# Modulation and c gradients of an adaLN block, taken from TensorE to ScalarE and VectorE

## The chip, the cores and the metric

The kernel runs on one core of a Trainium2 chip. The metric is device time in microseconds (us) of that core from launch to end; the median of three runs is compared. A separate, profiled execution gives the trace. Engines are named as in the profile: PE (TensorE matmuls; PEld its weight loads), DVE (VectorE), ACT (ScalarE), POOL (GpSimd), SP (the engine whose queue issues most DMAs).

## The reference

A transformer block with conditioning: a vector c gives six modulation rows, which shift, scale and gate an attention part and a dense part. The kernel computes the block's output and the gradients of nine inputs.

```python
mod = (silu(c) @ w_mod).reshape(1, 6, 1, 512)      # c 1x512, w_mod 512x3072
sa, ca, ga, sb, cb, gb = mod[:, 0..5]
h = layernorm(x) * (1 + ca) + sa
x = x + ga * attention(h, wqkv, wo)                # 2048 tokens, 32 heads of 16
h = layernorm(x) * (1 + cb) + sb
x = x + gb * dense(h, w1, b1, w2, b2)              # relu(.)^2, width 1792
out, vjp = jax.vjp(f, x, wqkv, wo, w1, b1, w2, b2, c, w_mod); grads = vjp(grad_out)
```

All inputs and outputs are bf16. What matters here are the last two gradients. With dmod the gradient of the six modulation rows (3072 numbers: sums over all tokens),

- the gradient of w_mod is the outer product silu(c)^T dmod, 512 x 3072 (out_9), and
- the gradient of c is silu'(c) * (w_mod dmod^T), 512 numbers (out_8).

## The kernel before, in words

Tokens are tiled by 128 (TT = 16 tiles), the width 512 by 128 (DC = 4). Most stages run under a schedule written out by hand: the order of instructions on PE, ACT and DVE is the program's own. In the last stage this holds for these three engines, while the order of SP's queue is made by the framework's scheduler. SP issues its DMAs in order; a DMA that has to wait for a semaphore holds all DMAs behind it. SP's DMAs also take turns on eight semaphores, so a DMA can't be issued before the eighth one ahead of it has landed.

The stages:

1. `prep` (lines 845 to 984, the first 41 us): loads, layer norm statistics, modulation columns, first keys and queries, four value tiles. Here SP also turns w_mod: `wmod_turn` (L911) issues four transposing DMAs of 128x512 for each of the first four sixths of w_mod into `tmpT`, and `wmod_store` (L917) writes them to the DRAM tile `wmT_st`. A row of c, its sigmoid and its product go to `rows_st` (L847, L867, L981 to L983).
2. Forward attention with exp on ACT (`ET`, L562), in units of four score matmuls and two ACTIVATEs. Tasks are hung on units: in the first twelve, `value_tile` (L815), which evicts a projection to `vP` on DVE (L822). `vP` has two buffers of four tiles, each written to `v_st` when full (L825), so tile t needs the store of tiles t-8 to t-5 to have landed. `later_stage` (L665) does weight turns at every fourth unit; for i of 30 and 31 the last two sixths of w_mod. At i = 25 the reciprocals of the two scale rows are stored to `rows_st`.
3. Dense part of the forward pass and its gradients, whose row sums over tokens end in `rows_st` rows 2 to 5 (L1533).
4. Attention gradients (most of the second half).
5. The last stage (from L1770, some 125 us): it turns the gradients of q, k, v to tokens (L1936), runs `dh1(t)` for 16 token tiles (12 matmuls, then DVE reductions, L1873), `row_sums(t)` (two matmuls against ones, L1893) and `dx_out(t)` (L1897), and then 12 products `dwqkv(b, ic)` of 16 matmuls each (L1906).

The gradients of w_mod and c are spread through stage 5. The late four rows (j = 2 to 5) come from `rows_st`, the first two (j = 0, 1) from the row sums after the last tile. `mod_cols` (L1838) turns each row of dmod into columns by four 1x1 matmuls. `c_grad` (L1845) multiplies those columns with the turned w_mod on PE, four matmuls a row. `wmod_grad` (L1850) makes the outer product on PE, a matmul with one contracted row for each 128x512 block, evicted by ACT into `dwms` and stored by SP.

Of the kernel before, what the change touches and what calls it, by code (L numbers as in the profile page):

```python
# [14 lines left out]
AF = mybir.ActivationFunctionType  # L15
ALU = mybir.AluOpType
AX = mybir.AxisListType
BF = dt.bfloat16
# [16 lines left out]
def kernel(  # L35
# [46 lines left out]
    rows_st = dram.tile([11, D], F32, name="rows_st")  # L82
# [15 lines left out]
    wmT_st = dram.tile([6, P, 4, D], BF, name="wmT_st")  # L98
# [48 lines left out]
    with ExitStack() as ph:  # L147
# [29 lines left out]
        def sp(to, fro, transpose=False):  # L177
            SP.dma_start(out=to, in_=fro, transpose=transpose)  # L178

        def later(lag, f, *args):  # L180
            due.append((unit[0] + lag, f, args))
# [483 lines left out]
        def later_stage(i):  # L665
# [22 lines left out]
            if i >= 26:  # L688
                j = i - 26
                wT = tmpT[:, 4 * (j % 2):4 * (j % 2) + 4, :]  # L690
                for q in range(4):
                    sp(wT[:, q, :], w_mod[:, (4 * j + q) * P:(4 * j + q + 1) * P], True)
                later(3, sp, wmT_st[j], wT)
                return
            if i == 25:
                for r, j in enumerate((1, 4)):
                    DVE.reciprocal(racc[0:1, r, :], modbc[0:1, j, :])
                later(3, sp, rows_st[9:11, :].unsqueeze(0), racc[0:1, 0:2, :])
                return
# [145 lines left out]
        def prep():  # L845
            cbf, crows = racc[0:1, 3, 0:256].bitcast(BF), racc[0:1, 0:3, :]
            sp(c_col, c.rearrange("o (ic p) -> p (o ic)", p=P))  # L847
            sp(cbf, c[0:1, :])
# [18 lines left out]
            ACT.activation(crows[:, 1, :], cbf, AF.Sigmoid)  # L867
# [43 lines left out]
            def wmod_turn(j):  # L911
                for q in range(4):
                    sp(tmpT[:, 4 * (j % 2) + q, :], w_mod[:, (4 * j + q) * P:(4 * j + q + 1) * P], True)
                if j > 0:
                    wmod_store(j - 1)

            def wmod_store(j):  # L917
                sp(wmT_st[j], tmpT[:, 4 * (j % 2):4 * (j % 2) + 4, :])

            for j in range(4):  # L920
                wmod_turn(j)
            wmod_store(3)
# [58 lines left out]
            POOL.tensor_copy(crows[:, 0, :], cbf)  # L981
            POOL.tensor_tensor(crows[:, 2, :], crows[:, 0, :], crows[:, 1, :], ALU.mult)
            sp(rows_st[6:9, :].unsqueeze(0), crows)  # L983
# [786 lines left out]
    with ExitStack() as ph:  # L1770
# [4 lines left out]
        psw = ph.enter_context(tc.tile_pool(name="psJw", bufs=2, space=bass.MemoryType.PSUM))  # L1775
        psk = ph.enter_context(tc.tile_pool(name="psK", bufs=1, space=bass.MemoryType.PSUM))
# [21 lines left out]
        def row(i):  # L1798
            r = big.tile([1, D], F32, name="row", tag="row", bufs=5)
            SP.dma_start(out=r[:], in_=rows_st[i:i + 1, :])  # L1800
            return r

        load_x(0)
        rows = {i: row(i) for i in (2, 5, 3, 4, 10)}
        load_x(1)
        wmodT = {}

        def load_wmodT(j):
            wmodT[j] = big.tile([P, 4, D], BF, name="wmodT", tag="wmodT", bufs=3)
            SP.dma_start(out=wmodT[j][:], in_=wmT_st[j])  # L1810
# [7 lines left out]
        siluc_rowbf = big.tile([1, D], BF, name="siluc_rowbfK")  # L1818
        dfac = big.tile([1, D], F32, name="dfac")
        dmodbf = big.tile([1, 6, D], BF, name="dmodbf")  # L1820
        dmodT = big.tile([P, 24], BF, name="dmodT")
        pdc = psk.tile([P, D], F32, name="pdc", tag="pdc")
        pc = psk.tile([P, 24], F32, name="pcolK", tag="pcolK")

        def silu_rows():
            DVE.tensor_copy(siluc_rowbf[:], rows[8][:])
            DVE.tensor_scalar(dfac[:], rows[7][:], -1.0, 1.0, ALU.mult, ALU.add)
            DVE.tensor_tensor(dfac[:], rows[6][:], dfac[:], ALU.mult)
            DVE.scalar_tensor_tensor(out=dfac[:], in0=dfac[:], scalar=1.0, in1=rows[7][:], op0=ALU.add, op1=ALU.mult)

        def mod_grad_rows(js, srcs):
            for j, src in zip(js, srcs):
                if j in (2, 5):
                    DVE.tensor_copy(dmodbf[:, j, :], src)
                else:
                    DVE.tensor_tensor(dmodbf[:, j, :], src, rows[9 if j < 2 else 10][:], ALU.mult)

        def mod_cols(js):  # L1838
            for j in js:
                for q in range(4):  # L1840
                    PE.matmul(pc[:, 4 * j + q:4 * j + q + 1], dmodbf[0:1, j, q * P:(q + 1) * P], ones_bf[0:1, 0:1],
                              start=True, stop=True)
            DVE.tensor_copy(dmodT[:, 4 * js[0]:4 * js[-1] + 4], pc[:, 4 * js[0]:4 * js[-1] + 4])

        def c_grad(j, first, last):  # L1845
            for q in range(4):
                PE.matmul(pdc[0:1, :], dmodT[:, 4 * j + q:4 * j + q + 1], wmodT[j][:, q, :],
                          start=(first and q == 0), stop=(last and q == 3))

        def wmod_grad(js, ic, lo, hi, pool, tag):  # L1850
            dwm = dwms[:, ic % 2]
            for i, j in list(enumerate(js))[lo:hi]:
                pw = pool.tile([P, D], F32, name="pwm", tag=tag)
                PE.matmul(pw[:], siluc_rowbf[0:1, ic * P:(ic + 1) * P], dmodbf[0:1, j, :], start=True, stop=True)
                ACT.activation(dwm[:, i, :], pw[:], AF.Identity)
            if hi < len(js):
                return
            SP.dma_start(out=out_9[ic * P:(ic + 1) * P, js[0] * D:(js[-1] + 1) * D].rearrange("p (j d) -> p j d", d=D),
                         in_=dwm[:, 0:len(js), :])

        dwms = stg.tile([P, 2, 4, D], BF, name="dwms", tag="dQacc", bufs=1)
        late_js = (2, 3, 4, 5)
# [30 lines left out]
        def row_sums(t):  # L1893
            for acc, src in zip(rsums, dxs[t]):
                PE.matmul(acc[0:1, :], ones_bf[:, 0:1], src[:], start=(t == 0), stop=(t == TT - 1))
# [31 lines left out]
        with tc.manual_schedule(engines={PE.engine, ACT.engine, DVE.engine}):  # L1927
# [17 lines left out]
            mod_grad_rows(late_js, [rows[j][:] for j in late_js])  # L1945
# [3 lines left out]
            for t in range(TT):  # L1949
                if t % 2 == 0 and t >= 2 and t // 2 + 2 < TT // 2:  # L1950
                    load_x(t // 2 + 2)
                if t in (0, 1, 2, 4, 6, 7):
                    load_wmodT({0: 2, 1: 3, 2: 4, 4: 5, 6: 0, 7: 1}[t])
                if t in (8, 9, 10, 11):
                    load_h1(t - 8)
                if t + 1 < TT:
                    norm_tile(t + 1)
                dh1(t)
                if t > 0:
                    row_sums(t - 1)  # L1960
                    dx_out(t - 1)
                if t == 0:
                    for i in (8, 7, 6, 9):
                        rows[i] = row(i)
                if t == 4:
                    silu_rows()
                if t == 1:
                    mod_cols(late_js)
                if 3 <= t < 7:
                    c_grad(t - 1, t == 3, False)  # L1970
                if 7 <= t < 15:
                    wmod_grad(late_js, (t - 7) // 2, 2 * ((t - 7) % 2), 2 * ((t - 7) % 2) + 2, psw, "pw")
            for b in range(3):
                for ic in range(DC):
                    dwqkv(b, ic)
                    i = b * DC + ic
                    if i == 0:
                        row_sums(TT - 1)
# [8 lines left out]
                    if i == 6:  # L1987
                        dcbf = wk.tile([1, D], BF, name="dcbf", bufs=1)
                        DVE.tensor_tensor(dcbf[:], pdc[0:1, :], dfac[:], ALU.mult)
                        SP.dma_start(out=out_8[0:1, :], in_=dcbf[:])  # L1990
# [61 lines left out]
```

## Time and profile before

| what | us |
|---|---|
| median of 3 runs | 2512.56 (2511.92 to 2516.4) |
| profiled execution, span | 2513.8 |
| PE busy | 2335.0 (93%) |
| ACT busy | 2302.6 (92%) |
| DVE busy | 1809.7 (72%) |
| POOL busy | 348.0 (14%) |
| start until the first `ET` | 41.71 |
| last stage, first `dh1` matmul to last product's last matmul | 2403.7 to 2510.0 |

The page's parts: busy time of each engine; the span in 40 slices; DMA queues; the chain of work that ended last, followed back from the last instruction to what released each step; groups of instructions with their mean duration and the idle time before them; DMA issues. The chain and the timeline can be asked for in a window of time. A line of the timeline has start, duration, engine, line, operation, output <- input, shapes, count, and in brackets the idle time of that engine just before, with what ended it. "SPq" is SP's queue while it issues or waits. Matmul durations in the trace are latencies: 128x512 matmuls show 0.38 us but follow each other by 0.216 us.

### The profile page before, as it was taken

Reading aid. Unit: us, or ns where it says so; the run is one execution under the profiler, and the core shown is the slowest. Engines: PE = TensorE matmul, PEld = TensorE weight load, DVE = VectorE, ACT = ScalarE, POOL = GpSimd, SP = SyncE. Lnnn points to the kernel's source line nnn. Section 1 sums busy time; section 2 is a strip of 40 time slices with the busy share of each in tenths; the row PEclk is TensorE's granted clock in tenths of the full one; section 3 lists DMA queues with packets and bytes.
Section 4 is the critical chain, followed back from the end, with each engine's and each line's share of the span. In section 5 each row is a group of like instructions: output and inputs, shape, how many; then the busy total and the mean of one; then the engine's idle time right before and its main releaser. Section 6 shows DMA issues by size and latency. Waiting matters only on the chain.

```text
span 2513.8 us, 49777 instructions
## 1 busy us (share of the span) xinstructions
PE 2335.0 (93%) x18916; PEld 777.9 (31%) x19005; DVE 1809.7 (72%) x2317; ACT 2302.6 (92%) x3577; POOL 348.0 (14%) x370
## 2 busy tenths in 40 slices
PE   7898889989988998999999999999999999999999
PEld 3232223222322323442233322233222323222343
DVE  6555153455435454579999999999998999999872
ACT  7999999999999999539999999999999999999952
POOL 2000000210333142210111101011010110110100
PEclk9999999999999999999999999999999999999999
DMA  6476465356748765969999999999999999999972
GB/s 203 129 193 177 136 131 139 96 160 136 110 88 174 153 131 118 264 211 184 207 203 210 199 198 204 204 201 206 204 200 206 199 195 204 206 199 215 197 254 72
DMA packets 1220981, 447.15 MB, mean 178 GB/s; under 512 B 1096951, under 2 KB 1191607, under 8 KB 1220486
## 3 DMA queue, kind: packets, MB, share of 16 engines
q1 hardware_dynamic: 1192822, 409.11, 81.8%
q0 software_dynamic: 10944, 16.78, 4.5%
q10 hardware_dynamic: 16976, 18.07, 2.8%
q8 instruction: 149, 2.44, 0.4%
q14 instruction: 90, 0.74, 0.1%
HBM read 96.75 MB, written 73.95 MB: 68 GB/s over the span
## 4 chain that ended last, share of the span: by engine, by line
PE 40%; ACT 39%; issue 7%; DVE 7%; DMA 4%; SPq 2%; ACTq 1%; POOL 0%; DVEq 0%; another core or an unknown queue 0%
ACT E_u L1601 24%; ACT ET L562 11%; PE dqacc L1682 5%; PE psST L560 4%; PE psS_A L1595 3%; PE pm L233 3%; PE accVK L1655 2%; ACT dsT L1761 2%; PE oacc L576 2%; PE psS_B L1595 2%; SPq L178 2%; PE psS_C L1595 2%; PE pm L412 2%; PE pdh L1876 2%; PE pwq L1910 2%
## 5 line engine op out<-in xcount | busy, mean ns | idle before, releaser
L1617 DVE TENSOR_TENSOR dS_u<-psD_u,E_u 128x1024 bf16<-128x1024 f32 x1024 | 1186.2, 1219 | 71.2 <-PE psD_u L1615 25.5
L562 ACT ACTIVATE ET<-psST 128x1024 bf16<-128x1024 f32 x1024 | 942.3, 1247 | 25.3 <-PE psST L560 24.7
L1601 ACT ACTIVATE E_u<-psS_A 128x512 bf16<-128x512 f32 x768 | 509.6, 664 | 11.0 <-PE psS_C L1595 8.5
L1601 ACT ACTIVATE E_u<-psS_B 128x512 bf16<-128x512 f32 x768 | 502.6, 654 | 12.5 <-PE psD_u L1615 3.4
L1615 PE MATMUL psD_u<-iv,ido 32*128 32x512 bf16 x2048 | 409.9, 388 | 0.5 <-DVE dS_u L1617 0.2
L560 PE MATMUL psST<-qt_sb,kt_sb 32*128 32x512 bf16 x2048 | 316.5, 387 | 53.0 <-ACT ET L562 46.2
L1601 ACT ACTIVATE E_u<-psS_C 128x512 bf16<-128x512 f32 x512 | 333.7, 652 | 2.7 <-PE psS_B L1595 1.0
L1595 PE MATMUL psS_B<-ik,iq 32*128 32x512 bf16 x768 | 294.9, 384 | 12.5 <-ACT E_u L1601 5.0
L1595 PE MATMUL psS_A<-ik,iq 32*128 32x512 bf16 x768 | 293.4, 382 | 11.1 <-DVE dwlast L237 1.0
L1595 PEld LDWEIGHTS <-iq 32*128 32x128 bf16 x2048 | 130.5, 91 | 316.0 <-issue 299.9
L1655 PE MATMUL accVK<-dS_u,qz 128*32 128x512 bf16 x2048 | 213.0, 390 | 0.5 <-PE psD_u L1615 0.3
L576 PE MATMUL oacc<-ET,vaug 128*32 128x512 bf16 x2048 | 207.8, 396 | 1.9 <-DVE ostage L580 1.9
L1664 PE MATMUL accVK<-E_u,dOs_tok 128*16 128x512 bf16 x2048 | 203.7, 386 | 0.0
L1700 POOL TENSOR_TENSOR dQacc<-dQacc,dqtmp 128x512 f32<-128x512 f32 x64 | 81.3, 1271 | 851.4 <-ACT dqtmp L1695 851.4
L1595 PE MATMUL psS_C<-ik,iq 32*128 32x512 bf16 x512 | 194.6, 380 | 4.2
L560 PEld LDWEIGHTS <-kt_sb 32*128 32x128 bf16 x2048 | 85.4, 91 | 341.0 <-issue 320.4
L1682 PE MATMUL dqacc<-dsT,KS_tok 128*32 128x512 bf16 x2048 | 147.7, 387 | 18.7 <-DMA dsT<-dS_u 4.3
L1761 ACT ACTIVATE dsT<-ptT 128x1024 bf16<-128x1024 bf16 x128 | 145.3, 1135 | 7.0 <-PE ptT L1645 6.4
L251 DVE COPY part<-pm 128x512 f32<-128x512 f32 (+2 forms) x103 | 63.5, 617 | 117.5 <-PE pm L233 106.0
L1615 PEld LDWEIGHTS <-ido 32*128 32x128 bf16 x2048 | 105.0, 91 | 100.7 <-issue 94.5
L1655 PEld LDWEIGHTS <-qz 128*32 128x32 bf16 x2048 | 58.5, 94 | 177.8 <-issue 162.8
L576 PEld LDWEIGHTS <-vaug 128*32 128x32 bf16 x2048 | 53.0, 93 | 121.0 <-issue 121.0
(407 smaller groups left out, 2499.5 us busy)
## 6 DMA issues: line engine op xcount, KB each, us to landing
p_st<-part POOLq DMA_DIRECT2D x36, 256.0 KB, 5.2
kt_sb<-qkT_st SPq DMA_DIRECT2D x124, 64.0 KB
wA<-in_B_w_dram SPq DMA_DIRECT2D x28, 256.0 KB
wB<-w1T_st SPq DMA_DIRECT2D x21, 256.0 KB
wA<-w2T_st SPq DMA_DIRECT2D x21, 256.0 KB
wB<-in_B_w_dram SPq DMA_DIRECT2D x21, 256.0 KB
p_st<-part POOLq DMA_DIRECT2D x25, 192.0 KB, 4.2
p_st<-part SPq DMA_DIRECT2D x18, 256.0 KB
```

Of the source, the lines that this page charges most:

```text
L560: PE.matmul(ps[:, hi, :], kt_sb[r:r + 32, kt * P:(kt + 1) * P], qt_sb[r:r + 32, :], start=True, stop=True, tile_position=(r, 0))
L562: ACT.activation(ET[:, 2 * pair:2 * pair + 2, :], ps[:], AF.Exp, scale=SCALE)
L576: PE.matmul(oacc[32 * hq:32 * hq + 32, :], lhsT, ET[:, hq, :], start=(kt == 0), stop=(kt == TT - 1), tile_position=(0, 32 * hq), skip_grou ...
L1595: PE.matmul(psS[:], st["q"][r:r + 32, qt * P:(qt + 1) * P], st["k"][r:r + 32, kc * 512:kc * 512 + 512], start=True, stop=True, tile_positi ...
L1601: ACT.activation(bst[u][0][:, hq, :], sst.pop((u, hq))[:], AF.Exp, scale=SCALE)
L1615: PE.matmul(psD[:, hi, :], st["do"][r:r + 32, qt * P:(qt + 1) * P], st["v"][r:r + 32, kc * 512:kc * 512 + 512], start=True, stop=True, til ...
L1617: DVE.tensor_tensor(dS_u[:, 2 * pair:2 * pair + 2, :], psD[:], E_u[:, 2 * pair:2 * pair + 2, :], ALU.mult)
L1655: PE.matmul(cur["vk"][32 * hq:32 * hq + 32, :], hst[hg]["qz"][:, qt, hq, :], bst[u][1][:, hq, :], start=(qt == 0), stop=False, tile_positi ...
L1664: PE.matmul(acc[32 * hq:32 * hq + DH, :], dOs_tok[:, qt, (hg * 4 + hq) * DH:(hg * 4 + hq + 1) * DH], E_u[:, hq, :], start=False, stop=(qt ...
L1682: PE.matmul(acc[32 * hq:32 * hq + 32, :], KS_tok[:, kc * 4 + kt, h * DH:h * DH + 32], tT[:, :, hq * 4 + kt, :], start=(kt == 0), stop=(kt ...
L1700: POOL.tensor_tensor(dst2, dst, tmp[:], ALU.add)
L1761: ACT.activation(dst, pt[:], AF.Identity)
```

## The change

- `prep` no longer loads c as a row, no longer turns w_mod, and stores no rows of c. Instead POOL makes `colc` (128x8 fp32, in columns): silu(c) and its derivative.
- `later_stage(30)` and `(31)` return without doing anything; the tile `wmT_st` is gone, `rows_st` has 8 rows.
- In the last stage the five single rows, and four more, are replaced by one DMA that reads rows 2 to 7 of `rows_st` and writes them to all 128 partitions (`sums`, 128 x 3072 fp32, 1.5 MB).
- `row_sums` multiplies with a 128x128 matrix of ones, so that the sums stand on all partitions.
- dmod stands on all partitions (`dmod`, bf16). `wmod_grad(k, h)` is one ACTIVATE of 128x1536 with a scale per partition, instead of matmuls and evictions; `c_grad(k, h)` is one DVE multiply-and-reduce of 128x1536 against natural rows of w_mod. Both run eight times, after products 1 to 8.
- `c_out` adds the halves, multiplies with the derivative, turns 128x4 to 4x128 on PE after product 9, and stores.
- PSUM: the pool of two banks for `mod_cols` and `c_grad` is gone, products get three banks instead of two.

```diff
-    rows_st = dram.tile([11, D], F32, name="rows_st")
+    rows_st = dram.tile([8, D], F32, name="rows_st")
+    colc = persist.tile([P, 8], F32, name="colc")
...
             if i >= 26:
-                j = i - 26
-                wT = tmpT[:, 4 * (j % 2):4 * (j % 2) + 4, :]
-                for q in range(4):
-                    sp(wT[:, q, :], w_mod[:, (4 * j + q) * P:(4 * j + q + 1) * P], True)
-                later(3, sp, wmT_st[j], wT)
                 return
...
-            sp(cbf, c[0:1, :])
...
-            ACT.activation(crows[:, 1, :], cbf, AF.Sigmoid)
...
-            for j in range(4):
-                wmod_turn(j)
-            wmod_store(3)
...
-            POOL.tensor_copy(crows[:, 0, :], cbf)
-            POOL.tensor_tensor(crows[:, 2, :], crows[:, 0, :], crows[:, 1, :], ALU.mult)
-            sp(rows_st[6:9, :].unsqueeze(0), crows)
+            POOL.tensor_copy(colc[:, 0:4], siluc_col)
+            POOL.tensor_scalar(colc[:, 4:8], sig_col, -1.0, 1.0, ALU.mult, ALU.add)
+            POOL.tensor_tensor(colc[:, 4:8], colc[:, 4:8], c_col, ALU.mult)
+            POOL.tensor_scalar(colc[:, 4:8], colc[:, 4:8], 1.0, None, ALU.add)
+            POOL.tensor_tensor(colc[:, 4:8], colc[:, 4:8], sig_col, ALU.mult)
...
         load_x(0)
-        rows = {i: row(i) for i in (2, 5, 3, 4, 10)}
         load_x(1)
...
+        sums = big.tile([P, 6, D], F32, name="sums_bc")
+        SP.dma_start(out=sums[:], in_=rows_st[2:8, :].unsqueeze(0).to_broadcast([P, 6, D]))
+        dmod = big.tile([P, 6, D], BF, name="dmod_bc")
+        wms = {}
+
+        def load_wmod(k, h):
+            wms[k, h] = big.tile([P, 3 * D], BF, name="wmodJ", tag="wmodJ", bufs=3)
+            SP.dma_start(out=wms[k, h][:], in_=w_mod[k * P:(k + 1) * P, 3 * D * h:3 * D * h + 3 * D])
 
         load_x(2)
...
+        def late_mods():
+            for j in (2, 5):
+                ACT.activation(dmod[:, j, :], sums[:, j - 2, :], AF.Identity)
+            for j in (3, 4):
+                DVE.tensor_tensor(dmod[:, j, :], sums[:, j - 2, :], sums[:, 5, :], ALU.mult)
+
+        def wmod_grad(k, h):
+            part = slice(3 * D * h, 3 * D * h + 3 * D)
+            dst = dwms[:, h, :]
+            ACT.activation(dst, dmod.rearrange("p j d -> p (j d)")[:, part], AF.Identity, scale=colc[:, k:k + 1])
+            SP.dma_start(out=out_9[k * P:(k + 1) * P, part], in_=dst)
+
+        def c_grad(k, h):
+            part = slice(3 * D * h, 3 * D * h + 3 * D)
+            prod = wk.tile([P, 3 * D], BF, name="cprod", tag="cprod", bufs=1)
+            DVE.tensor_tensor_reduce(out=prod[:], in0=wms.pop((k, h))[:], in1=dmod.rearrange("p j d -> p (j d)")[:, part],
+                                     scale=1.0, scalar=0.0, op0=ALU.mult, op1=ALU.add, accum_out=ccols[:, k, h:h + 1])
+
+        def c_out():
+            dc = wk.tile([P, 4], F32, name="dc", bufs=1)
+            DVE.tensor_tensor(dc[:].unsqueeze(2), ccols[:, :, 0:1], ccols[:, :, 1:2], ALU.add)
+            DVE.tensor_tensor(dc[:], dc[:], colc[:, 4:8], ALU.mult)
+            pc = psd.tile([P, D], F32, name="pdc", tag="pdh1")
+            PE.transpose(pc[0:4, 0:P], dc[:], identf[:])
+            dcbf = wk.tile([4, P], BF, name="dcbf", bufs=1)
+            ACT.activation(dcbf[:], pc[0:4, 0:P], AF.Identity)
+            SP.dma_start(out=out_8.rearrange("o (ic p) -> (o ic) p", p=P), in_=dcbf[:])
...
-                PE.matmul(acc[0:1, :], ones_bf[:, 0:1], src[:], start=(t == 0), stop=(t == TT - 1))
+                PE.matmul(acc[:], ones_bf[:], src[:], start=(t == 0), stop=(t == TT - 1))
...
-                if t in (0, 1, 2, 4, 6, 7):
-                    load_wmodT({0: 2, 1: 3, 2: 4, 4: 5, 6: 0, 7: 1}[t])
+                if t in (4, 6, 7):
+                    load_wmod({4: 0, 6: 0, 7: 1}[t], {4: 0, 6: 1, 7: 0}[t])
...
-                if t == 1:
-                    mod_cols(late_js)
-                if 3 <= t < 7:
-                    c_grad(t - 1, t == 3, False)
-                if 7 <= t < 15:
-                    wmod_grad(late_js, (t - 7) // 2, 2 * ((t - 7) % 2), 2 * ((t - 7) % 2) + 2, psw, "pw")
...
                     if i == 0:
                         row_sums(TT - 1)
                         dx_out(TT - 1)
-                        mod_grad_rows((0, 1), [rsums[j][0:1, :] for j in range(2)])
-                    if i == 2:
-                        mod_cols((0, 1))
-                    if i in (4, 5):
-                        c_grad(i - 4, False, i == 5)
-                    if 5 <= i < 9:
-                        wmod_grad((0, 1), i - 5, 0, 2, psd, "pdh1")
...
+                        late_mods()
+                        for j in range(2):
+                            DVE.tensor_tensor(dmod[:, j, :], rsums[j][:], sums[:, 4, :], ALU.mult)
+                    elif i <= 2 * DC:
+                        k, h = (i - 1) // 2, (i - 1) % 2
+                        wmod_grad(k, h)
+                        c_grad(k, h)
+                        if i + 2 < 2 * DC:
+                            load_wmod((i + 2) // 2, i % 2)
+                    if i == 2 * DC + 1:
+                        c_out()
```

More of the change, by code (lines that the diff above doesn't have):

```diff
@@ L97 @@
     wT_st = dram.tile([12, P, D], BF, name="wT_st")
-    wmT_st = dram.tile([6, P, 4, D], BF, name="wmT_st")
     h1_st = dram.tile([P, TT, D], BF, name="h1_st")
@@ L697, in later_stage @@
                     DVE.reciprocal(racc[0:1, r, :], modbc[0:1, j, :])
-                later(3, sp, rows_st[9:11, :].unsqueeze(0), racc[0:1, 0:2, :])
+                later(3, sp, rows_st[6:8, :].unsqueeze(0), racc[0:1, 0:2, :])
                 return
@@ L845, in prep @@
         def prep():
-            cbf, crows = racc[0:1, 3, 0:256].bitcast(BF), racc[0:1, 0:3, :]
             sp(c_col, c.rearrange("o (ic p) -> p (o ic)", p=P))
-            sp(cbf, c[0:1, :])
             for g in range(QC):
@@ L909, in padded_proj @@
                     PE.matmul(acc, w[:, ic].rearrange("p h c -> p (h c)"), h1Ts[g][:, ic, :], start=(ic == 0), stop=(ic == DC - 1))
[L911 to L918, printed above, removed]
-            for j in range(4):
-                wmod_turn(j)
-            wmod_store(3)
             stats_tiles(0, range(4))
@@ L1774 @@
         psd = ph.enter_context(tc.tile_pool(name="psJd", bufs=2, space=bass.MemoryType.PSUM))
-        psw = ph.enter_context(tc.tile_pool(name="psJw", bufs=2, space=bass.MemoryType.PSUM))
-        psk = ph.enter_context(tc.tile_pool(name="psK", bufs=1, space=bass.MemoryType.PSUM))
+        psw = ph.enter_context(tc.tile_pool(name="psJw", bufs=3, space=bass.MemoryType.PSUM))
         xs["dq", 1], xs["dq", 2], xs["vk", 4], xs["vk", 5] = (hsets[1][key] for key in ("q", "k", "v", "do"))
@@ L1796, in load_x @@
             SP.dma_start(out=dx1s[g][:], in_=dx1_st[:, 2 * g:2 * g + 2, :])
[L1798 to L1801, printed above, removed]
         load_x(0)
-        rows = {i: row(i) for i in (2, 5, 3, 4, 10)}
         load_x(1)
[L1806 to L1810, printed above, removed]
+        sums = big.tile([P, 6, D], F32, name="sums_bc")
[5 more added lines that the diff above has]
+            SP.dma_start(out=wms[k, h][:], in_=w_mod[k * P:(k + 1) * P, 3 * D * h:3 * D * h + 3 * D])
         load_x(2)
@@ L1816, in load_h1 @@
             SP.dma_start(out=h1J[:, 4 * g:4 * g + 4, :], in_=h1_st[:, 4 * g:4 * g + 4, :])
[L1818 to L1859, printed above, removed]
@@ L1861 @@
-        dwms = stg.tile([P, 2, 4, D], BF, name="dwms", tag="dQacc", bufs=1)
-        late_js = (2, 3, 4, 5)
+        ccols = big.tile([P, 4, 2], F32, name="ccols")
+        def late_mods():
[3 more added lines that the diff above has]
+                DVE.tensor_tensor(dmod[:, j, :], sums[:, j - 2, :], sums[:, 5, :], ALU.mult)
+        dwms = stg.tile([P, 2, 3 * D], BF, name="dwms", tag="dQacc", bufs=1)
@@ L1944 @@
                         ACT.activation(dst, pt[:], AF.Identity)
-            mod_grad_rows(late_js, [rows[j][:] for j in late_js])
             norm_tile(0)
@@ L1961 @@
                     dx_out(t - 1)
[L1962 to L1966, printed above, removed]
-                if t == 1:
-                    mod_cols(late_js)
-                if 3 <= t < 7:
-                    c_grad(t - 1, t == 3, False)
-                if 7 <= t < 15:
-                    wmod_grad(late_js, (t - 7) // 2, 2 * ((t - 7) % 2), 2 * ((t - 7) % 2) + 2, psw, "pw")
             for b in range(3):
@@ L1979 @@
                         dx_out(TT - 1)
-                        mod_grad_rows((0, 1), [rsums[j][0:1, :] for j in range(2)])
-                    if i == 2:
-                        mod_cols((0, 1))
-                    if i in (4, 5):
-                        c_grad(i - 4, False, i == 5)
-                    if 5 <= i < 9:
-                        wmod_grad((0, 1), i - 5, 0, 2, psd, "pdh1")
[L1987 to L1990, printed above, removed]
+                        late_mods()
[9 more added lines that the diff above has]
+                        c_out()
     stg.release()
```

## The prediction

> **What bounds the kernel now.** I read the page's engine table first: PE 93%, ACT 92%, DVE 72% are means over stages with different limits, so I asked for the chain of waits only in the two stretches the change edits, the start (0 to 75 us) and the last stage (from 2360 us).
>
> The chain at the start (start us, us, what):
>
> ```profile
> by line: SPq L178 49.0%; ACT ET L562 22.4%; DMA wmT_st<-tmpT 11.5%; DMA v_st<-vP 6.0%; issue 4.9%; PE pm L817 3.8%; PE psST L560 1.2%; DVE vP L822 0.9%; PE oacc L576 0.7%; DVEq L822 0.0%
> ...
> 25.57 2.79 DMA wmT_st<-tmpT
> ...
> 47.92 4.53 DMA v_st<-vP
> 52.54 0.70 DVE vP L822
> 53.28 1.86 PE pm L817 x4
> ```
>
> To be seen: SP is the path. From 13.20 to 43.3 it issues or waits for the turned w_mod, so the first value store goes out only at 47.92 and lands at 52.45. The fifth value tile (t = 8) reuses that buffer, and DVE stands for it. The same moment in the order of time, for SP, DVE and ACT:
>
> ```profile
> 13.20 12.18 SPq L178 DMA_TRANSPOSE tmpT<-in_w_mod_dram  x8
> ...
> 47.92 1.59 SPq L178 DMA_DIRECT2D v_st<-vP  x2
> ```
> ```profile
> 52.54 0.69 DVE L822 CAST vP<-pm 128x512 bf16<-128x512 f32 x1 [2.90 <-DMA v_st<-vP]
> ```
> ```profile
> 41.71 11.11 ACT L562 ACTIVATE ET<-psST 128x1024 bf16<-128x1024 f32 x12 [3.46 <-PE psST L560]
> 55.79 20.29 ACT L562 ACTIVATE ET<-psST 128x1024 bf16<-128x1024 f32 x22 [2.98 <-PE psST L560]
> ```
>
> ACT runs without a gap before and after (0.92 us each), so its 2.98 us are lost to the whole kernel.
>
> The last stage, by the chain:
>
> ```profile
> by line: PE pdh L1876 26.5%; PE pwq L1910 26.2%; DMA wT_all<-wT_st 7.2%; ACT E_u L1601 5.9%; PE rsumJ L1895 5.3%; PE pwm L1854 4.0%; PE pdc L1847 3.4%; DMA dsT<-dS_u 3.3%; issue 2.8%; PE dqacc L1682 2.6%; DVE dS_u L1617 2.4%; SPq L1632 0.9%
> ...
> 2409.57 0.48 PE pcolK L1841 x16
> ...
> 2413.26 2.70 PE pdh L1876 x12
> 2415.96 0.52 PE rsumJ L1895 x2
> 2416.49 0.86 PE pdc L1847 x4
> ...
> 2432.82 0.53 PE pwm L1854 x2
> ```
>
> From 2403.7 to 2510 nearly every piece is PE. So PE time taken out here shortens the end, as long as nothing else takes over.
>
> **Part 1, PE work leaves the last stage.** From the chain's pieces: pcolK 0.48 + 0.28 = 0.76; pdc 4 x 0.86 + 2 x 0.95 = 5.34; pwm eleven pairs of 0.53 and one of 0.60 = 6.43. Sum 12.5 us, of which 8.15 lie between the 16 dh1 tiles and 4.4 between the 12 dwqkv products. Does another engine take over? A dh1 tile without extras takes PE 2.70 + 0.52 = 3.22 us; DVE, in such a tile (2412.78 to 2416.00), works 2.86 and stands 0.36; ACT works 1.6. PE stays the bound, narrowly. In dwqkv a product takes PE 3.5 us. ACT gains one 128x1536 ACTIVATE for each of eight products: iqs 128x1024 took 1.05 and the constant 128x2048 1.90, so 0.83 ns an element, 1.5 us, plus 0.2 for the pointer scale (tqa took 0.81 where a plain 512 took 0.60): 1.7, with its eviction of 0.60 2.3 of 3.5. DVE gains eight products of 128x1536: 512 took 0.69 + 0.08, and evictions of 256 and 512 (0.425, 0.69) give 1.04 ns an element, so 1.8 us each, with the 0.42 eviction 2.3 of 3.5. The conversions of six rows (four DVE at 0.68, two ACT at 0.6 to 0.8) run while PE is in products 0 and 1, and nobody on PE waits for them. They are hidden by PE; without that cover they'd cost 8 x 1.8 = 14 us.
>
> Row sums on 128 rows: same 512 columns streamed, weights load 0.098 instead of 0.080 us, hidden behind the matmul before (0.216 apart). I take 0; ends 0 and 32 x 0.018 = 0.6.
>
> **Added wait.** c_out puts a PE transpose after product 9, and it waits for DVE. Before product 9 is evicted DVE can't reach it: at the end of the trace PE stops at 2509.98 and DVE's eviction ends at 2510.84, 0.86 later; two 128x4 operations (0.16 each) and the hand-overs make 1.2; the fp32 transpose 0.1 to 0.5. Products 10 and 11 are queued behind it on PE, so all of it counts: 1.2 to 1.8, I take 1.4. An idle PE could also lose its clock. Rows: after 1.78 us of idle (2402.81) the transposes ran at the same 0.056 us spacing as before; after 2.45 us (53.28) four matmuls took 1.86 instead of 1.04. 1.4 is on the safe side, price 0, other end 0.8. The Trainium skill ("TensorE: Matmul & The Clock Gate", The HAM clock gate) puts the gate at an idle window of about 3.4 us; the 2.45 us row contradicts a plain reading of it, and by the page this stall would also cost nothing.
>
> Part 1: -12.5 + 1.4 = -11.1 us.
>
> **Part 2, SP at the start.** Removed: 16 transposes (about 1.26 each on the queue), four stores, three waits of 2.8 to 2.9, the c row load and the rows store. The first v_st then waits only for DVE's fourth value tile (41.2) and, at the same 4.5 us, lands at 45.8, where DVE wants the buffer at about 50.0. Next late could be the second store (buffer of t = 4 to 7): ready at 49, landed 53.5, wanted at 57. So the stall goes and nothing nearer replaces it: -2.98. The c row load stood ahead of x on SP (0.44); the first bn_stats waits for x and the first pcol for w_mod, so -0.4 (ends 0 and -0.44). On POOL two 1x512 operations (0.60, 1.26) become five of 128x4 (0.2 to 0.3 each). DVE beside the old ones took 2.15 for two xnP instead of 0.73, and 0.45 of that could reach the path; I take 0. One-row sigmoid 0.61 on ACT lay in a wait: 0. The two turns at 159 to 174 us lay where ACT has no gap: 0.
>
> Part 2: -3.4 us.
>
> **Part 3, the sums broadcast.** One DMA of 128 x 12 KB = 1.57 MB replaces nine 2 KB rows, and w_mod comes in eight natural pieces of 384 KB instead of six of 512. In the changed program's SP order the broadcast stands after x pair 1 and ahead of x pair 2, three w_mod pieces and h1. It starts at about 2404. At the 299 to 341 GB/s this queue moved from 2390 to 2402 it takes D = 5 us; at the fastest slice (418) 3.8; at the kernel's mean (178) 8.8. Who waits: the tightest is dx1 of pair 3, which waits for the store of pair 0, queued behind some 2.65 MB after the broadcast and ahead of 1 MB of h1. At 0.3 MB/us that is 8.8 and 3.3 us, and two landings add some 3 (v_st took 4.53 for 512 KB, 1.7 of it at that rate): it lands at about 2404 + D + 15 = 2419 + D; DVE wants it for tile 6 at 2403.7 + 8 x 3.22 = 2429.5. So D up to 10 us is free, and each further us costs about one, DVE first, then PE for want of a psd bank. I take 0. No row shows 128 reads of one address.
>
> The skill speaks against this part: "DMA: Bandwidth & Descriptors" (Latency and other measured facts) gives copies 103 GB/s where all partitions' rows fall together at large power-of-two pitches; pitch 0 may be like that. By the page D would be 15 us (my estimate) and the sum 5 worse.
>
> **Sum.** -11.1 - 3.4 = -14.5 us. The profiled execution's span, 2513.8, would become 2499.3. The span stands 1.2 over the median 2512.56, so the median becomes 2498.
>
> **Rivals.** (a) The head's stall only moves: the store of 512 KB takes as long to land and another wait (kt_sb of the next head, the second store) stands in its place. For it: SP still carries the q, k, bound and value stores and the next head's loads there; against: the 4 us of slack worked out above. -11.1 - 0.4: 2501. (b) Broadcast mildly slow, D of 11 to 20 us (80 to 140 GB/s): gives back 1 to 10, about 5: 2503. (c) Broadcast at 55 to 75 GB/s, D 21 to 29: no change, 2512. (d) Slower: the broadcast crawls because all engines read the same 12 KB. Place: SP's queue in the dh1 stage, dx1 and x behind it. Price: D - 10. It eats all gains from D = 25, and is a loss over 5 us from D = 30 (52 GB/s); at D = 35, 2523. For it: no such load anywhere in the trace; against: with loads of 1 KB packets and more queued, the stretches from 2390 to 2402 show nothing under 299 GB/s. That the change doesn't free PE is no rival: the built PE order has those matmuls gone and nothing but one transpose added.
>
> **How the numbers follow.** Main case 0.62: own range 2495 to 2501 (unknown terms +0.6, +0.4, +0.8, -0.45, and the three runs' scatter). (a) 0.12, (b) 0.12, (c) 0.07, (d) 0.07. 0.2%, 5 us, is about what a measurement of this kernel can tell from no change. Faster 0.62 + 0.12 + 0.12 = 0.86, within 0.07, slower 0.07. The range takes in main, (a) and (b): 2494 to 2507.
>
> **What would show it.** In the profile after: no gap in ET between 40 and 60 us, with v_st issued near 41 us; 3.2 us per dh1 tile throughout and ACT's xn1b never waiting for DMA; 3.5 us per product, with one PE gap of 1.2 to 1.8 us after product 9. The prediction is wrong if DVE or ACT waits for x0J or dx1J in the dh1 stage, if a product waits for a psw bank, or if the ET stage shows a new gap.

## The result, and the profile after

The changed kernel takes 2502.86 us (median of 17 runs, 2492.07 to 2512.69), the kernel before on the same chips 2514.43 us (17 runs, 2510.2 to 2524.71). The ratio is 0.9943, with a 95% interval of 0.9929 to 0.9957: 14.3 us less, between 10.8 and 17.9 (the two medians by themselves lie 11.6 apart, the means 13.9). The forecast was 14.5 us less. The total was right; two of its terms were not, and they were off in opposite directions. The experiments show this.

The profiled run of the changed kernel is the slowest of its 17 (span 2510.9 us), so the two spans say little, and the stages are compared one by one.

The start of the changed kernel, SP's queue in order of time (start us, us, instruction):

```profile
12.84 0.38 SPq L178 DMA_DIRECT2D tmpT<-in_A_wqkv_dram  x1
...
38.21 1.17 SPq L178 DMA_DIRECT2D m_st<-sP  x2
41.59 8.09 SPq L178 DMA_DIRECT2D v_st<-vP  x2
```

ScalarE in the same stretch (in square brackets the idle time before a group, and who ended it):

```profile
42.10 44.10 ACT L562 ACTIVATE ET<-psST 128x1024 bf16<-128x1024 f32 x48 [3.46 <-PE psST L560]
```

The turns of w_mod are gone from the queue, the first value store is issued at 41.59 instead of 47.92, and 48 exponentials now run without a gap where the 13th waited 2.98 us before. The first exponential itself is not earlier (42.10 against 41.71).

The chain of waits in the last stage, over its start:

```profile
2402.64 9.96 DMA qz<-dQst
2412.60 0.25 issue
2412.85 1.01 PE ptq L1901 x8
2413.86 0.85 PE ptd L1901 x8
2414.71 6.40 PE pdh L1841 x24
2421.12 0.43 PE rsumJ L1860 x2
2421.55 2.59 PE pdh L1841 x12
```

TensorE waits for the last small qz loads, comes out of the pause at about half clock (eight transposes in 1.01 us instead of 0.61, 24 matmuls in 6.40 instead of 5.18), and only then runs at 2.59 us per tile. The same chain through the 12 products:

```profile
2463.85 3.45 PE pwq L1875 x16
2467.31 0.43 PE rsumJ L1860 x2
2467.74 31.09 PE pwq L1875 x144
...
2498.85 0.39 ACT wqblk L1886
...
2499.27 0.42 DVE wqblk L1888
2499.70 0.08 DVE dc L1820
...
2499.80 0.17 DVE dc L1821
...
2500.01 0.27 PE pdc L1823
2500.29 6.92 PE pwq L1875 x32
```

Nine products run through in 31.09 us, 3.45 each, and no other engine takes over. Then the one added wait: from 2498.83 to 2500.01 TensorE stands for two evictions and two tiny VectorE operations, and the transpose itself follows. The two products after it take 3.46 us each, so 1.2 us of idle time cost no clock. What the other engines do instead, from the groups of instructions of this stretch (busy us, mean ns of one, idle before):

```profile
L1815 DVE CUSTOM_DVE_ANT_0 cprod<-wmodJ,dmod_bc 128x1536 bf16<-128x1536 bf16 x8 | 14.0, 1752 | 0.3
L1809 ACT ACTIVATE dwms<-dmod_bc,colc 128x1536 bf16<-128x1536 bf16 x8 | 12.6, 1569 | 1.3 <-DMA out_dram<-dwms 1.2
```

1.75 and 1.57 us (forecast 1.8 and 1.7), beside products of 3.45.

### The profile page after: what moved, and what is told of

Read it like the earlier page. It is cut to its first block, busy times and chain, and to the rows that moved or that the text cites. A ratio compares the mean times of both kernels' runs of the same rounds, so it can differ in the third digit from the quotient of the medians.

```text
span 2510.9 us, 49682 instructions
## 1 busy us (share of the span) xinstructions
PE 2336.8 (93%) x18934; PEld 778.5 (31%) x18934; DVE 1818.7 (72%) x2326; ACT 2304.1 (92%) x3563; POOL 348.1 (14%) x373
## 4 chain that ended last, share of the span: by engine, by line
PE 41%; ACT 39%; issue 7%; DVE 7%; DMA 4%; SPq 1%; ACTq 1%; DVEq 0%; POOL 0%; POOLq 0%
ACT E_u L1583 23%; ACT ET L562 12%; PE dqacc L1664 4%; PE psST L560 4%; PE psS_A L1577 3%; PE pm L233 3%; PE accVK L1637 2%; PE oacc L576 2%; PE psS_B L1577 2%; ACT dsT L1743 2%; DMA dsT<-dS_u 2%; PE psS_C L1577 2%; PE pm L398 2%; PE pm L412 2%; PE pdh L1841 2%
## 5 line engine op out<-in xcount | busy, mean ns | idle before, releaser
L1743 ACT ACTIVATE dsT<-ptT 128x1024 bf16<-128x1024 bf16 x128 | 144.8, 1131 | 11.5 <-PE ptT L1627 10.7
```

Source lines behind the costliest of these rows:

```text
L1743: ACT.activation(dst, pt[:], AF.Identity)
```

## The experiments

The time of one kernel spreads by 15 to 20 us over its 17 runs, so effects of 1 to 3 us are read from pieces of the trace. Three pieces serve. *Head blocks*: the 32 copies of an attention output (ostage from oacc, L580 on VectorE) are marks through the score stage. *Start of the last stage*: from the end of the last dqacc matmul to the first row sum. *Rest of the last stage*: from the first row sum (after the first two gradient tiles) to the end of the last product. "Early" is against the first profile of the kernel before.

**Row sums on 128 partitions, in the kernel before.**

```diff
-PE.matmul(acc[0:1, :], ones_bf[:, 0:1], src[:], start=...
+PE.matmul(acc[:], ones_bf[:], src[:], start=...
```

> The kernel before, its row sums written to 128 partitions (ones of 128 columns in place of one column), nothing else. Theory A (the one-column weight costs TensorE time, so the changed kernel's gain beyond the forecast in its gradient tiles comes from the wide sums): one tile of 12 + 2 matmuls goes from 3.22 to 3.02 us, 16 x 0.2 = 3.2 us less from the first gradient matmul to the last product matmul, 103 instead of 106.3. Theory B (my forecast's zero: the width costs nothing either way, and the tile gained from the other small matmuls having left): 3.2 us a tile as before, 106.3.

Measured: ratio 0.9984 (0.9968 to 1.0001). The rest of the last stage takes 99.66 us where all four profiles of the kernel before have 100.98 to 101.00: 1.33 us less, and 105.7 from the first gradient matmul on: neither theory's number, though theory A's sign. The chain of this run:

```profile
2424.07 2.59 PE pdh L1876 x12
2426.66 0.43 PE rsumJ L1895 x2
2427.09 0.95 PE pdc L1847 x4
2428.05 2.70 PE pdh L1876 x12
...
2446.65 0.43 PE rsumJ L1895 x2
2447.08 0.53 PE pwm L1854 x2
2447.61 2.70 PE pdh L1876 x12
```

And the changed kernel:

```profile
2442.70 2.59 PE pdh L1841 x12
2445.29 0.43 PE rsumJ L1860 x2
2445.72 2.59 PE pdh L1841 x12
```

Two wide row sums take 0.43 us where the one-column pair took 0.52. And twelve gradient matmuls take 2.59 us after a wide group, but 2.70 after pdc or pwm, whose weights are one column or one row. So each change between such a group and one with 128x128 weights costs about 0.1 us, outside the matmuls' own time (all are listed at 0.38). Between two groups of the same form nothing is lost: pdc, with one-column weights too, takes 0.86 us after the one-column sums and 0.95 after the wide ones. With the sums alone widened the small groups still break the run; with both gone a plain tile falls from 3.22 to 3.02 us. The same shows in the products: 3.56 us after a small group in the kernel before, 3.45 in the changed one.

**The c transpose one product later, in the changed kernel.**

```diff
                     if i == 2 * DC + 1:
+                        c_sum()
+                    if i == 2 * DC + 2:
                         c_out()
```

> The changed kernel, with the transpose of the c gradient one product later than the two vector operations that it reads (after the 11th product instead of the 10th). Theory (TensorE waits about 1.2 us for the c sums and nothing else is wrong there): no wait at the transpose, from the first gradient matmul to the last product matmul 92.5 - 1.3 = 91.2 us. Rival (the wait is for something else, as a free accumulator): the wait moves along with the transpose, 92.5.

Measured: ratio 0.9936 (0.9918 to 0.9953). The chain:

```profile
2462.78 34.53 PE pwq L1878 x160
2497.32 0.11 PE pdc L1826
2497.43 3.47 PE pwq L1878 x16
```

There is no wait; ten products run through and the transpose costs 0.11 us of the path. From the first gradient matmul on it is 91.74 us, but that has the scatter of the first two tiles in it. The rest of the last stage is 84.88 us, where the changed kernel's four profiles have 86.24 or 86.25: the wait was worth 1.36 us, and it came from the order alone.

**The four turns of the first stage moved, in the kernel before.**

```diff
-            for j in range(4):
-                wmod_turn(j)
-            wmod_store(3)
...
-stages = [*range(4, 14), *range(4), 30, 31, *range(14, 26)]
+stages = [*range(4, 14), *range(4), 26, 27, 28, 29, 30, 31, *range(14, 26)]
```

> The kernel before, with the four turns of w_mod (16 transposing loads and four stores) taken out of the first stage and done in the attention stage beside the other two; the last stage is that of before. Theory (the stores stood before the value store in the queue, and four score tiles waited for it): no idle stretch of near 3 us within the first 40 exponentials, the 256th exponential 2.5 to 3.2 us earlier counted from the first one, and nothing lost later: 2514.4 - 3 = 2511 us. Rival (the stall only moves: the four turns cost as much in the attention stage, or the chain there regains it anyway): the 256th exponential as early or late as before, 2514 us.

Measured: 2542.9 us, ratio 1.0094 (1.0072 to 1.0117), slower than both theories. The first 52 exponentials run without a gap, as the theory said, but SP's queue looks like this from 176 us on,

```profile
175.95 6.80 SPq L178 DMA_TRANSPOSE tmpT<-in_w_mod_dram  x4
...
188.59 5.11 SPq L178 DMA_TRANSPOSE tmpT<-in_w_mod_dram  x4
...
196.11 2.09 SPq L140 DMA_DIRECT2D kt_sb<-qkT_st  x4
198.24 1.81 SPq L140 DMA_DIRECT2D qt_sb<-qkT_st  x4
200.09 0.58 SPq L140 DMA_DIRECT2D qt_sb<-m_st  x1
```

and TensorE, in the same run:

```profile
202.15 0.71 PE L560 MATMUL psST<-qt_sb,kt_sb 32*128 32x512 bf16 x4 [11.53 <-DMA qt_sb<-m_st]
```

Each group of four transposing loads holds the queue for 5 to 7 us, and the next head's q and k loads, queued behind them, come 11.5 us late. In the kernel before, x loads of 0.4 to 1.4 us had this place. By the ninth block the run is 22.8 us late, by the 32nd 27. So this run doesn't isolate the head: it priced the place to which I moved the turns. It does show that a large delay here passes through to the end of the stage undiminished.

**The turns put back, in the changed kernel.** (In its first stage only; the four stores go to a scratch that nothing reads.)

```diff
+            for j in range(4):
+                wmod_turn(j)
+            wmod_store(3)
             stats_tiles(0, range(4))
```

> The changed kernel, with the four turns of w_mod and their four stores put back where they stood in the first stage (what they store is read by nothing). Theory (the head is worth 3 us, the rest 11): the idle stretch of near 3 us is back at the 38th exponential, 2502.9 + 3 = 2506 us. Rival (the whole gain is in the last stage): 2503 us. A third (the stall was the row store's, not the turns'): no idle stretch, 2503.

Measured: 2501.59 us, ratio 0.9934 (0.9915 to 0.9952). ScalarE:

```profile
41.82 11.11 ACT L563 ACTIVATE ET<-psST 128x1024 bf16<-128x1024 f32 x12 [3.46 <-PE psST L561]
55.33 4.89 ACT L563 ACTIVATE ET<-psST 128x1024 bf16<-128x1024 f32 x5 [2.40 <-PE psST L561]
```

The stall is back (at the 13th exponential, where it is in the first profile of the kernel before, not at the 38th as I had written) without the row store, so the third theory falls, and blocks 2 to 16 come 0.2 to 0.5 us early instead of the 2.5 to 4.4 of the changed kernel's first profile. But the run isn't slower than the changed kernel: the times side with the rival, the trace's early part with the theory. That is why the next runs look at what becomes of the lead.

**The broadcast ahead of the first x tiles, in the changed kernel.**

```diff
-        load_x(0)
-        load_x(1)
         sums = big.tile([P, 6, D], F32, name="sums_bc")
         SP.dma_start(out=sums[:], in_=rows_st[2:8, :].unsqueeze(0).to_broadcast([P, 6, D]))
+        load_x(0)
+        load_x(1)
```

> The changed kernel, with the broadcast load of the six sum rows put ahead of the first x and dx tiles instead of behind the second pair, so that its duration D is no longer covered and can be read from the first x tile's arrival. Theory (D is some 5 us, as the forecast took it from the weight load of the same 1.5 MB): the first normalization of x on ScalarE starts some 3 to 6 us later than in the changed kernel, counted from the last qz load's landing, and VectorE waits for it in the first tile, a few us in all. Rival (D is 15 us or more, the broadcast reads one row again and again): 13 us later or more, and the first two tiles stand still for about 10 us.

Measured: ScalarE, at the first normalization:

```profile
2394.81 1.02 ACT L1909 ACTIVATE dq_tok<-ptq 128x1024 bf16<-128x1024 bf16 x1 [6.63 <-PE ptq L1901]
2397.64 1.52 ACT L1834 ACTIVATE xn1b<-x0J,nb,rstd 128x512 bf16<-128x512 bf16 x2 [1.81 <-DMA x0J<-in_A_x_dram]
```

The last qz load lets TensorE go at 2393.76; 3.88 us later the broadcast and the first x tile (256 KB) are there, 13.6 us after the broadcast's issue at 2384.03. ScalarE waits 1.81 us and the rest of the stage is 86.24 us as ever. This doesn't give D by itself, as part of the broadcast moved before 2393.76. But the trace records every packet, and the broadcast is the only load with packets of 12 KB, 128 of them (the kernel before has none): here they run from 2389.41 to 2396.42, 7.0 us with 0.7 MB of other loads among them. In the changed kernel's four profiles, in later transpose, turns back and weights split, they take 5.2 to 6.1 us, 259 to 301 GB/s. So D is what the theory said, and the rival, 15 us, falls. (The run's 2492.97 us, one run, is a short gradient stage: 1253.9 us from the first E_u to the last dqacc matmul, which has nothing to do with this edit.)

**The weight load in five parts, qz between them, and the later transpose.**

```diff
-        SP.dma_start(out=wT[:], in_=wT_st.rearrange("j p d -> p j d"))
+        wT_v = wT_st.rearrange("j p d -> p j d")
+        for a, b in ((10, 12), (4, 8)):
+            SP.dma_start(out=wT[:, a:b, :], in_=wT_v[:, a:b, :])
         for h in range(4):
             SP.dma_start(out=xs["dq", 3][64 + DH * h:...
+        for a, b in ((0, 2), (8, 10), (2, 4)):
+            SP.dma_start(out=wT[:, a:b, :], in_=wT_v[:, a:b, :])
```

> The kernel of the run before (c transpose one product later) with the 1.5 MB weight load of the last stage in five parts in the order of use, and the last four small qz loads between the second and the third of them. Theory (the last stage starts late because the small loads that the last turns wait for stand behind the whole weight load in one queue, and the pause of over 4 us halves the clock after it): TensorE waits 1 to 2 us in place of 4 to 5 there, the turns and the first tiles run at full clock, from the last dqacc matmul to the last product matmul 3 to 4 us less (106.0 in the run before, 108.8 in the changed kernel): 102 to 103, and 2498 us. Rival (only the bytes count: all of the weights are needed before the first tile can end): the wait goes into the first tile, 105 to 106, 2501 us.

Measured: 2495.96 us, ratio 0.9927 (0.9908 to 0.9946). From the last dqacc matmul to the last product 102.4 us, as forecast. The chain:

```profile
2394.81 5.10 DMA wT_all<-wT_st
2399.91 0.61 PE ptq L1908 x8
2400.52 0.45 PE ptd L1908 x8
2400.96 5.18 PE pdh L1848 x24
```

TensorE's wait is 2.05 us here, and the transposes and the first two tiles run at full clock. It is the best version of this study in the trace; the changed kernel, timed beside it, had 0.9936 (0.9917 to 0.9956), so by their times the two can't be told apart.

**Both kernels again**, without an edit, for more profiles of each.

> The changed kernel once more. Theory (what it lost in its profile between 700 us and the last stage is scatter between executions): 2503 us, and in the profile the score stage's tiles before 700 us stand 2.5 to 3.5 us ahead of the kernel before again, while the loss after 700 us comes out different. Rival (the gain of the head is always given back there): the same places lose the same 3 to 5 us.

> The kernel before once more, for a second profile of it. Theory (scatter): its wait for the feed-forward weights near 724 us is in some executions long enough to halve the clock, in others not, so the 23rd head block can come 2 to 4 us later than in the first profile; the last stage from the first gradient matmul on takes 106.3 us again. Rival (only the changed kernel loses there): the same times as in the first profile within 0.5 us up to 1000 us.

> The changed kernel, a third profile. Theory (the head's lead is lost on the way): at the 9th head block it stands 2 to 4 us ahead of the kernel before's first profile, at the 32nd within 1 us of the mean of the looks at the kernel before, because TensorE, being early, waits longer for the second feed-forward weights near 724 us and its clock is halved there more often. Rival (the lead is kept, and the losses so far were chance): 2 us or more ahead at the 32nd block too.

> The kernel before, a third profile. Theory (lead lost): the 32nd head block at 1005 to 1009 us as in the looks with the turns in the first stage so far, no later than in the changed kernel. Rival (lead kept): it comes 2 us later than in the changed kernel's looks on the mean. The last stage, from the first gradient matmul to the last product matmul, again 106 to 107 us.

> The changed kernel, a fourth profile: as for the third. The last stage, from the first gradient matmul to the last product matmul, again 91.4 to 92.7 us, by whether the clock is halved at its start.

> The kernel before, a fourth profile: as for the third profile of it, with the 32nd head block no later than in the changed kernel (lead lost) or 2 us later (lead kept), and 106 to 107 us from the first gradient matmul to the last product matmul.

Measured, in the order of these six: 2499.21 us (ratio 0.9936, 0.9917 to 0.9956), and single runs of 2525.1, 2496.3, 2512.65, 2502.6 and 2514.93 us. The pieces, all in us, four profiles of each kernel:

| piece | before | changed |
|---|---|---|
| first exponential | 41.71, 42.77, 42.70, 41.49 | 42.10, 41.13, 42.28, 41.25 |
| first to last exponential | 964.2, 962.6, 961.7, 969.3 | 966.5, 965.5, 962.7, 968.7 |
| first E_u to last dqacc end | 1265.7, 1271.5, 1261.9, 1257.0 | 1270.8, 1268.2, 1258.8, 1261.8 |
| last dqacc end to first gradient matmul | 13.53, 17.03, 14.75, 15.09 | 16.16, 13.99, 16.27, 14.06 |
| the first two gradient tiles | 5.27, 5.84, 6.80, 7.32 | 6.44, 5.18, 6.01, 6.86 |
| first row sum to end of last product | 101.00, 100.98, 101.00, 100.99 | 86.24, 86.25, 86.24, 86.24 |

The last row is the change, to a hundredth: 14.75 us. The two rows above it are the clock and the loads at the start of the last stage; they scatter in both kernels (my 106 to 107 for the kernel before missed twice, 107.80 and 108.31, and my 91.4 to 92.7 for the fourth profile of the changed one, 93.10, by the two tiles at low clock alone). The gradient stage scatters over 14 us in the kernel before and 12 in the changed one; with the score stage it makes the spread of the run times.

The kernel before doesn't always stall at the start. Its second profile, ScalarE:

```profile
42.77 42.44 ACT L562 ACTIVATE ET<-psST 128x1024 bf16<-128x1024 f32 x46 [3.46 <-PE psST L560]
```

The first exponential is 1.1 us later than in the first profile and nothing stops the next 45, though the value store is issued at 47.90 as before; in the third profile it is the same but for 0.34 us. Their first head blocks come 1.9 and 1.6 us earlier than that of the first profile. The stall is there in the first and the fourth (2.77 us), and in wide sums and turns back (1.50 and 2.40).

For the head, the six profiles with the turns in the first stage (before four times, wide sums, turns back) stand against the seven without (changed four times, later transpose, sums first, weights split). Means, with the standard error of the difference:

| head block | with turns | without | difference |
|---|---|---|---|
| 1st | 75.28 | 73.19 | -2.1 ± 0.4 |
| 9th | 318.68 | 316.76 | -1.9 ± 0.5 |
| 22nd | 703.79 | 702.05 | -1.7 ± 1.1 |
| 24th | 765.73 | 764.54 | -1.2 ± 1.5 |
| 25th | 799.83 | 799.69 | -0.1 ± 1.3 |
| 32nd | 1007.73 | 1007.88 | +0.2 ± 1.2 |

So the head is worth 2 us for 300 us, and at the end of the stage nothing that these 13 profiles can tell from zero; 2 us are not excluded either. Taken singly the last profiles went both ways: the third profile of the changed kernel was 1.91 us early at the ninth block, 0.05 at the 22nd and 0.95 at the 32nd (1.7 ahead of the mean of the four of before); the fourth went from 3.9 early at the ninth to 4.0 late at the 32nd. My forecast for the second profile of the kernel before, its 23rd block 2 to 4 us later than in the first, missed: it came 1.2 us earlier.

Where some of it goes, TensorE of the changed kernel's first profile shows:

```profile
724.86 1.01 PE L487 MATMUL pm<-wB,sT 128*128 128x512 bf16 x2 [2.39 <-DMA wB<-in_B_w_dram]
...
729.85 1.87 PE L487 MATMUL pm<-wB,sT 128*128 128x512 bf16 x4 [0.41 <-DVE ftmp L497]
```

It waits for the second feed-forward weights, and then four matmuls take 1.87 us instead of 1.02. By stretches of time (busy time of each engine, then the granted clock, DMA share, GB/s):

```profile
722.00:728.00 6.00, 3.61 (x18) 0.68 (x17) 0.00 (x0) 2.98 (x4) 0.00 (x0) 0.67 1.14 302
728.00:732.00 4.00, 3.59 (x17) 0.72 (x12) 2.17 (x3) 2.38 (x3) 1.15 (x1) 0.50 0.02 4
732.00:736.00 4.00, 4.00 (x24) 1.06 (x20) 0.00 (x0) 2.99 (x4) 0.00 (x0) 0.71 0.00 0
```

The clock is halved for some 10 us (724.1 to 734.3), and the exponentials wait for TensorE four times (3.02, 0.56, 1.44 and 0.63 us). In the 13 profiles this divides by the lead at the 22nd block, not by the kernel: the five that are 1.77 us early or more (changed three times, later transpose, and wide sums, which has the turns) wait 2.1 to 3.2 us in all for these weights, have the clock halved there for 3.4 to 10.2 us, and end the stage 0.7 to 4.0 us late, 2.3 on the mean. Of the eight that are less early, seven (one with the clock halved there) end 1.5 early to 2.0 late, 0.2 early on the mean; the eighth (before, fourth) was already 4.8 late. TensorE's last wait for these weights ends at 724.9 to 725.9 in the five and at 725.6 to 728.0 in the seven: 1.2 us earlier on the mean, with a lead 1.9 larger. So only part of the lead is met by an earlier load, and a longer wait goes with the halved clock. That is a pattern in 13 profiles, with a bound set after seeing them; no run changed this load to prove it.

By the table part of the lead goes later, between the 24th and 25th blocks (1.0 ± 0.9 us there, 0.6 ± 1.0 from the 22nd to the 24th). There TensorE waits for a transposing load,

```profile
797.13 1.89 PE L347 MATMUL pm<-wo_nat,OT 128*128 128x512 bf16 x4 [2.86 <-DMA OT<-O_c]
```

1.1 to 5.3 us in 12 of the 13 profiles (not in the late one; 2.4 on the mean with the turns, 2.9 without), and the clock is halved in all 12. What makes this wait differ, no run shows. My wording in the expectations, that the clock near 724 us tells the two kernels apart, doesn't hold: it sank between 724 and 736 us in three of six profiles with the turns and in four of seven without.

## Why the prediction was right, and where it was not

*PE work out of the last stage, -12.5: mis-sized.* The mechanism holds, and nothing took over: VectorE waits 0.16 us per tile for TensorE, no product waits for a bank. With the added wait taken off, the removal measured 14.75 + 1.36 = 16.1 us. The step that failed is "Row sums on 128 rows: same 512 columns streamed, [...] I take 0", with ends at 0 and +0.6: I compared the weight loads of the two forms and saw that the wider one is hidden. I did not compare the matmuls' spacing on either side of a small group, which was in the chain: 0.52 for two row sums against 0.43 for any two matmuls of 0.216. Widening alone is worth 1.33 us; the remaining 2.3 of the 3.6 come from the small groups, which cost, beyond their own pieces, 0.1 us for the return to 128x128 weights.

*Added wait of c_out, 1.4 (1.2 to 1.8), no loss of clock: right.* 1.36 us, shown by moving it away (the 0.11 of the transpose itself stays); full clock after it.

*The head, -3.4: the stall went, but no gain is seen at the end of the stage.* The gap of 2.98 us went as worked out, the first store was issued at 41.59 (forecast 41), and its place was not taken by the second store. The 0.4 us for the c row load can't be seen: the first exponential comes at 42.05 us on the mean of the five profiles with that load (before four times, wide sums) and at 41.93 in the eight without, each over a range of 1.3 us. The step that failed is "ACT runs without a gap before and after (0.92 us each), so its 2.98 us are lost to the whole kernel". I took one profile for the kernel: two of its four have no stall. And ScalarE runs without a gap around the stall, but not near 724 and 795 us, where TensorE waits for loads; the first block is 2.1 us earlier on the mean, the 32nd 0.2 ± 1.2 later, three standard errors from the forecast. What causes the loss stays open. Rival (a), "the head's stall only moves", is nearer to what the end of the score stage shows; the lead goes further on than I looked.

*VectorE and ScalarE operations, hidden: right.* 1.75 and 1.57 us against 1.8 and 1.7.

*Broadcast, D = 5 us and 10 free: right.* By its packets it takes 5.2 to 6.1 us (7.0 where I moved it ahead of the x tiles). The Trainium skill's 103 GB/s for copies with row pitches of 4 and 8 MiB ("DMA: Bandwidth & Descriptors", Latency and other measured facts) does not describe 128 reads of the same row here: the packets show 259 to 301 GB/s. Rivals (b), (c) and (d) fall with it. "ACT's xn1b never waiting for DMA" held in the changed kernel.

*The sum.* -14.75 in the last stage and about 0 in the head make the measured 14.3, where -11.1 and -3.4 made 14.5. The total was right by luck: two errors of some 3.5 us, in opposite directions, cancelled, as far as the ± 1.2 us on the head lets one say.

## What to carry to other kernels

Cost a small matmul not by its own piece but by the difference between two tiles with and without it: a group with one-column or one-row weights also costs the matmuls around it. A stall removed early need not be worth its length at the end: look in a second profile whether it is always there, and follow the engine through the later waits to the end of the stage before booking it. And where a step is moved, price the queue at the new place: the four groups of transposing loads cost up to 3 us in the first stage, and 27 by the end of the attention stage when moved there.

## What I had not expected of the hardware

The last stage after its first two tiles repeats to 0.02 us, while the loads and the clock ahead of it move by 4. The clock is not decided by one pause alone: after 2.05 us (weights split) and after 0.76 + 1.49 us (before, first profile, near 725 us) it stayed full, in a pause of 2.39 us it was halved, and in the second profile of the kernel before it was halved for 3.4 us in the second of two pauses of 0.80 and 0.83 us, with matmuls between them. In all 14 profiles the clock is either full or half, and within each profile every change lies on a grid of 3.41 us, whose offset differs from profile to profile: halved stretches last 3.4, 6.8, 10.2 us and so on. So where a pause falls on that grid may matter as well as its length; no run tests this. The Trainium skill's idle window of about 3.4 us ("TensorE: Matmul & The Clock Gate", The HAM clock gate) is longer than the pauses of 2.39 and 0.83 us in which it was lowered here.
